# Moving small VectorE work of a fused attention and expert kernel to GpSimd, and scaling early probabilities at their way out of PSUM

## The chip, the cores and the metric

The kernel runs on one core of a Trainium2 chip. Its engines are TensorE (PE in the profile; PEld is its weight load), VectorE (DVE), ScalarE (ACT), GpSimd (POOL) and SyncE (SP), which here only issues transfers. The metric is device microseconds of one launch, the median over several runs; lower is better.

## What is computed

`reference` chains three parts over 4 sequences of 576 tokens with 512 channels.

- **Attention**: 8 heads of 64 channels. Scores are q·k/8 under a block-causal mask (a query sees its own block of 64 and all earlier ones), then a softmax with 1e-9 added to the sum, then the product with v.
- **A dense block** on its result x: `x + relu(layernorm(x) * g @ w_ch1) @ w_ch2`, 512 to 2048 to 512 channels.
- **Experts**: 8 experts of 512 to 1024 to 512 channels; each token takes the expert of the largest logit, or that of the token before it when its local gate says so; the result is scaled by that expert's probability.

## The kernel before

**Numbers.** Operands of TensorE are fp16 pairs: a high half (a cast) and a low half (the fp32 value less the high half). Values v are scaled by V_S = 256, and probabilities by P_S = 256, so that the low halves stay in fp16's range. Before, P_S enters the exponential as LOG_P = ln 256 added to its bias, for every head.

**Tiles.** The 2304 tokens are 18 tiles of 128, in the order 0 to 17. A step s is one tile and one head: 144 steps. The steps of one tile go through `qk` (scores into PSUM), `maxes` (L324 on DVE: scale, mask, row extreme into `sums`; L328 adds LOG_P to the extreme), `exps` (L335 on ACT: exponential, row sums into `sums`), a transposition of the probabilities, and `pv` (times the values). In steps below 30 (`early`: all of tiles 0 to 2, and the first six heads of tile 3) the transposition is done by TensorE in fp32: `emit_turns` transposes into PSUM (L366), ACT writes the high half from there (L369), DVE the low half (L370). In later steps ACT and POOL make the halves (L350, L353, zeros at L352) and a transfer on SP's queue transposes them (L356).

**`finish`** closes a tile after its last `pv`. L408 (DVE) turns the row sums into `(sum + P_S * 1e-9) * V_S`, L411 (DVE) takes the reciprocal, L414 (POOL) multiplies the tile with it. L421 to L426 (DVE) are mean, variance and a first guess of 1/sqrt; L431 (DVE) normalizes by that guess; L435 (ACT) and L436 (POOL) make the halves, and a transfer (L440, SP) transposes them for the dense block. L449 to L468 (DVE) are seven operations on one column that refine the guess to a factor `fac`, read by `post` after the second product.

**Loads and splits.** `load_tile` issues q, k and v of a tile on SP's queue; v has one buffer (`RB = 1`), q and k two. `split_q` and `split_k` make halves on ACT (L237, L244) and POOL (L238, L245; of the first tile on DVE). `split_v` makes the high half on ACT (L252), scaled by V_S, and the low half on DVE (L253, `v * V_S - high` in one operation). They are called in steps 3 and 6 of the tile before.

**Dense weights.** The inputs w_ch1 and w_ch2 are float64. In the first 18 steps `w_next` takes 32 pieces of them: three integer operations on DVE build an fp32 (L198, L202, L205), ACT scales and casts (L218, L219), POOL makes the low half (L223). When a tile group has finished, its dense block is queued in quanta: `l1` (L486 to L488, output halves by ACT L490 and DVE L491) and `l2` (L508 to L510, then `post`, L514 to L526). Quanta are dealt out among the steps by their cost.

**The order.** Every engine works through its own queue in order, and so does each transfer queue. The operations up to the first step are issued in the order of the code; from there to the end of attention a planner that simulates the engines puts each engine's instructions into an order, with priority to tiles 0 and 1 (`HT = 2`). The part after attention (routing and experts) has an order written out by hand for the compute engines.

Of the kernel before, what the change touches and what calls it, by code (L numbers as in the profile page):

```python
# [14 lines left out]
AF = mybir.ActivationFunctionType  # L15
ALU = mybir.AluOpType
# [6 lines left out]
B, H, S, D = 4, 8, 576, 64  # L23
# [11 lines left out]
V_S = 256.0  # L35
P_S = 256.0
LOG_P = math.log(P_S)
# [5 lines left out]
ORDER = [i for ts in GROUPS for i in ts]  # L43
# [47 lines left out]
def kernel(  # L91
# [14 lines left out]
    nc = tc.nc  # L106
# [140 lines left out]
    def split_v(i):  # L247
        r = raw.pop(("v", i))
        o = (KRING + turn_v[0] % VRING) * 1024
        turn_v[0] += 1  # L250
        n = spare[:, o:o + 1024].rearrange("p (h e d) -> p h e d", h=H, e=2)
        nc.scalar.activation(out=n[:, :, 0], in_=r, func=AF.Copy, scale=V_S)  # L252
        nc.vector.scalar_tensor_tensor(  # L253
            out=n[:, :, 1], in0=r, scalar=V_S, in1=n[:, :, 0],
            op0=ALU.mult, op1=ALU.subtract,
        )
        vt[i] = n

    def keys(i):
# [19 lines left out]
    def pack(i):  # L279
        return {1: 2, 2: 2}.get(len(keys(i)), 1)  # L280
# [26 lines left out]
    def early(s):  # L307
        return s < FEW * H - 2

    def maxes(i, h):  # L310
        lo, n = span(i)
        m = pack(i)
        sp = sps.pop((i, h))
        mask = mask_m if i % 9 == 4 else mask_a
        if h % m == 0:
            if early(step[0] + pack(i) - 1):
                sms[i] = ring("ph", [P, 10 * P], F16, 3, MPH).bitcast(F32)
            else:
                sms[i] = ring("sm", [P, 5 * P], F32, 2, MSM)
        sm = sms[i][:, h % m * n:(h % m + 1) * n]  # L320
        if h == 0:
            sums[i] = at.tile([P, 2, H], F32, tag="sums", name="sums", bufs=2)
        nm = sums[i][:, 0, h:h + 1]
        nc.vector.tensor_tensor_reduce(  # L324
            out=sm[:, lo:n], in0=sp[:, lo:n], in1=mask[:, 5 * P - n + lo:5 * P],
            scale=-0.125, scalar=3.0e38, op0=ALU.add, op1=ALU.min, accum_out=nm,
        )
        nc.vector.tensor_scalar(out=nm, in0=nm, scalar1=LOG_P, scalar2=None, op0=ALU.add)  # L328

    def exps(i, h):  # L330
        lo, n = span(i)
# [29 lines left out]
    def emit_turns(upto):  # L361
        while turns and turns[0][0] <= upto:
            _, sm, t, m, k = turns.pop(0)
            tp = sctx["p"].tile([P, 4, P], F32, tag="t", name="ps_t", bufs=2)
            for c in range(m * k):
                nc.tensor.transpose(tp[:, c], sm[:, c * P:(c + 1) * P], eye)  # L366
            tp = tp[:, :m * k].rearrange("p (m k) c -> p m k c", m=m)
            t = t[:, :2 * m * k].rearrange("p (m e k) c -> p m e k c", m=m, e=2)
            nc.scalar.copy(out=t[:, :, 0], in_=tp)  # L369
            nc.vector.tensor_tensor(out=t[:, :, 1], in0=tp, in1=t[:, :, 0], op=ALU.subtract)  # L370

    obs = {}

# [31 lines left out]
    def finish(i):  # L405
        sv = sums.pop(i)
        r = at.tile([P, H], F32, tag="rinv", name="rinv", bufs=2)
        nc.vector.tensor_scalar(  # L408
            out=r, in0=sv[:, 1], scalar1=P_S * 1e-9, scalar2=V_S, op0=ALU.add, op1=ALU.mult
        )  # L410
        nc.vector.reciprocal(out=r, in_=r)  # L411
        ob = obs.pop(i)
        x = wp.tile([P, H, D], F32, tag="x", name="x", bufs=6)
        nc.gpsimd.tensor_tensor(  # L414
            out=x, in0=ob, in1=r[:, :, None].to_broadcast([P, H, D]), op=ALU.mult
        )
        x = x.rearrange("p h d -> p (h d)")
        xt[i] = x
        sm = at.tile([P, 12], F32, tag="lns", name="lns", bufs=2)
        mean, var, y, w = (sm[:, c:c + 1] for c in (6, 7, 8, 9))  # L420
        nc.vector.bn_stats(out=sm[:, 0:6], in_=x)  # L421
        nc.vector.bn_aggr(out=sm[:, 6:8], in_=sm[:, 0:6])
        nc.vector.tensor_scalar(out=var, in0=var, scalar1=LN_EPS, scalar2=None, op0=ALU.add)


        nc.vector.tensor_scalar(  # L426
            out=y.bitcast(I32), in0=var.bitcast(I32), scalar1=-0.5, scalar2=1597463007.0,
            op0=ALU.mult, op1=ALU.add,
        )
        xn = at.tile([P, DM], F32, tag="ob", name="xn", bufs=2)  # L430
        nc.vector.tensor_scalar(  # L431
            out=xn, in0=x, scalar1=mean, scalar2=y, op0=ALU.subtract, op1=ALU.mult
        )
        xh = at.tile([P, 2, DM], F16, tag="nat", name="xh", bufs=2)
        nc.scalar.copy(out=xh[:, 0], in_=xn)  # L435
        nc.gpsimd.tensor_tensor(out=xh[:, 1], in0=xn, in1=xh[:, 0], op=ALU.subtract)  # L436
        g, j, n = group_of(i)
        if j == 0:
            xg[g] = wp.tile([P, 2 * KD, n * P], F16, tag="xg", name="xg", bufs=2)
        nc.sync.dma_start_transpose(  # L440
            out=xg[g][:, :, j * P:(j + 1) * P], in_=xh.rearrange("p e d -> p (e d)")
        )
        if i in GROUPS[-1]:
            c = GROUPS[-1].index(i)
            nc.vector.tensor_copy(stats[:, c, 0:1], mean)
            nc.vector.reciprocal(out=stats[:, c, 1:2], in_=y)

        f = fac[:, i:i + 1]
        nc.vector.scalar_tensor_tensor(  # L449
            out=w, in0=y, scalar=var, in1=y, op0=ALU.mult, op1=ALU.mult  # L450
        )
        nc.vector.tensor_scalar(
            out=f, in0=w, scalar1=-1.0, scalar2=3.0, op0=ALU.mult, op1=ALU.add
        )
        nc.vector.scalar_tensor_tensor(
            out=y, in0=f, scalar=w, in1=f, op0=ALU.mult, op1=ALU.mult
        )
        nc.vector.scalar_tensor_tensor(
            out=f, in0=y, scalar=12.0, in1=f, op0=ALU.subtract, op1=ALU.mult
        )  # L460
        nc.vector.scalar_tensor_tensor(
            out=y, in0=f, scalar=w, in1=f, op0=ALU.mult, op1=ALU.mult
        )
        nc.vector.tensor_scalar(
            out=y, in0=y, scalar1=HOUT / 8192.0, scalar2=HOUT * -3.0 / 32.0,
            op0=ALU.mult, op1=ALU.add,
        )
        nc.vector.tensor_tensor(out=f, in0=f, in1=y, op=ALU.mult)  # L468


    todo = []

# [22 lines left out]
    op = {}  # L495
# [263 lines left out]
    for s in range(nsteps + LAG + MPT):  # L759
# [9 lines left out]
        if s < nsteps:  # L769
            i, h = steps[s]  # L770
# [9 lines left out]
            t = s // H  # L780
# [21 lines left out]
        if queue:  # L802
# [5 lines left out]
            while acc > 0 or s < FREE:  # L808
                n = [x for x in queue if need(x) <= wpos[0] - WREADY]
                n = [x for x in n if x[0] == "l1" or x[1:] == l2_at[0] or x[3] == 0 and l2_free()][:1]  # L810
# [19 lines left out]
    def whole(name, shape, pattern, mult=0, base=0, dt=F32):  # L830
# [17 lines left out]
        out=c_tri16, in_=c_one16, pattern=[[1, P]], compare_op=ALU.is_gt, fill=0.0,  # L848
# [10 lines left out]
    for b in range(B):  # L859
        t, r = divmod(b * S, P)  # L860
# [233 lines left out]
    def third(n):  # L1094
# [14 lines left out]
        out=cand, in0=sub, scalar=0.0, in1=bc(c_rev[:, None, :], NTILE, NE),  # L1109
        op0=ALU.is_equal, op1=ALU.mult,  # L1110
# [6 lines left out]
        out=fresh, in0=z, scalar=0.0, in1=c_first, op0=ALU.is_lt, op1=ALU.max  # L1117
# [15 lines left out]
        out=scan, data0=c_one[:NTILE], data1=pt1[:NTILE, :P], initial=0.0,  # L1133
        op0=ALU.mult, op1=ALU.max,
# [14 lines left out]
        out=car[:, 1:], data0=c_one[:1, :NTILE], data1=pt2[:1, :NTILE], initial=0.0,  # L1149
        op0=ALU.mult, op1=ALU.max,  # L1150
# [14 lines left out]
        out=oh, in0=bc(c_exp[:, :, None], NE, NTILE), in1=bc(ef[:, None, :], NE, NTILE),  # L1165
        op=ALU.is_equal,
# [6 lines left out]
        out=inc.rearrange("p e t -> p (e t)"), data0=c_seg.rearrange("p e t -> p (e t)"),  # L1173
# [6 lines left out]
        out=exc16, in0=inc.rearrange("p e t -> p (e t)"), in1=ohf, op=ALU.subtract  # L1180
    )
    early = GROUPS[last][0]
# [11 lines left out]
        out=lack, in0=pt5[:, NE:NE + 1], scalar1=-1.0, scalar2=128.0, op0=ALU.mult, op1=ALU.add  # L1194
# [5 lines left out]
        out=nti[:, 0:1], in0=pt5[:, 0:1], scalar1=lack, scalar2=127.0, op0=ALU.add, op1=ALU.add  # L1200
# [6 lines left out]
        out=endc, data0=c_one[:, :NE], data1=ntf, initial=0.0, op0=ALU.mult, op1=ALU.add  # L1207
# [6 lines left out]
        out=dst3, in0=pt6[:, :NE * NTILE].rearrange("p (e t) -> p e t", e=NE),  # L1214
        in1=bc(base[:, :, None], NE, NTILE), op=ALU.add,
    )
    V.tensor_scalar(
        out=dst3[:, 0, early:], in0=dst3[:, 0, early:], scalar1=lack, scalar2=None, op0=ALU.add
# [3 lines left out]
    with nc.allow_low_precision("whole numbers"):  # L1222
        V.tensor_reduce(
            out=dst, in_=dst3.rearrange("p e t -> p t e"), axis=AX.X, op=ALU.add
# [21 lines left out]
        out=val[:, :, 0], in0=bc(c_slot[:, None, :], NTILE, NSLOT),  # L1246
        in1=bc(slotf[:, :, None], NTILE, NSLOT), op=ALU.is_equal,
    )
    for n, w in ((1, c_tile), (2, c_row), (3, gh), (4, gl)):
        V.tensor_tensor(  # L1250
            out=val[:, :, n], in0=val[:, :, 0], in1=bc(w[:, :, None], NTILE, NSLOT), op=ALU.mult
# [3 lines left out]
    for t in range(NTILE):  # L1255
        pick = ep.tile([P, P], F16, tag="pick", name="pick", bufs=4)
        V.tensor_scalar(
            out=pick, in0=c_iota, scalar1=rowf[:, t:t + 1], scalar2=None, op0=ALU.is_equal
# [165 lines left out]
```

## Time and profile before

| | us |
|---|---|
| median of 3 runs (lowest, highest) | 811.77 (810.96, 815.51) |
| the profiled execution's own time | 818.86 |
| its span, first to last instruction | 817.2 |
| busy: TensorE, VectorE | 727.9, 431.4 |
| busy: ScalarE, GpSimd | 378.4, 327.9 |

The mean granted TensorE clock is 0.96 of full speed. A window view gives, for stretches of the span, how long each engine was busy; a group view gives one line's instructions of one shape with their number, total and mean time, and behind the bar the idle time of the engine just before them; a timeline gives start and duration of single instructions. Durations in a timeline overlap: a short VectorE instruction is reported somewhat longer than the distance to the start of the next. Attention and the dense block fill the span up to about 520 us, the routing and the experts the rest.

### The profile page before, as it was taken

The numbers are of one execution on the slowest core, as the hardware profiler recorded it, in microseconds if no ns is written. First come the engines' busy times: TensorE is split into PE (matmuls) and PEld (weight loads), VectorE is DVE, ScalarE is ACT, GpSimd is POOL, SyncE is SP. The second block draws the span as 40 slices with busy tenths as digits, with TensorE's granted clock in tenths as the row PEclk, the third lists the DMA queues.
The fourth block names the chain that finished last, engine by engine and source line by source line (L and its number), as shares of the span: only waits on it lengthen the run. The fifth ranks groups of instructions, "written<-read, shape, count | busy, mean of one in ns | idle before, by whom it ended". The sixth has DMA issues, their size and how long they took to land.

```text
span 817.2 us, 16334 instructions
## 1 busy us (share of the span) xinstructions
PE 727.9 (89%) x5598; PEld 435.6 (53%) x5598; DVE 431.4 (53%) x1234; ACT 378.4 (46%) x843; POOL 327.9 (40%) x344
## 2 busy tenths in 40 slices
PE   2559648979998999999999999998997999999995
PEld 1337415676856857656655665455453444444442
DVE  7999986456546467566556653486781111111110
ACT  6878667655546447567554651363051111111110
POOL 3753586756256346566555542300021111111110
PEclk9998778999999999999999999998998999999998
DMA  8874555977478479688966754594025567555663
GB/s 309 294 221 130 155 188 125 222 159 164 63 143 168 124 169 199 117 163 160 194 112 141 120 99 87 180 368 136 14 70 126 124 127 127 121 126 123 131 126 75
DMA packets 240782, 122.60 MB, mean 150 GB/s; under 512 B 220272, under 2 KB 220272, under 8 KB 240688
## 3 DMA queue, kind: packets, MB, share of 16 engines
q1 hardware_dynamic: 233600, 97.05, 55.7%
q10 hardware_dynamic: 3888, 14.16, 5.3%
q0 software_dynamic: 3200, 10.23, 3.9%
q8 instruction: 49, 0.80, 0.4%
q14 instruction: 45, 0.37, 0.1%
HBM read 138.17 MB, written 9.70 MB: 181 GB/s over the span
## 4 chain that ended last, share of the span: by engine, by line
PE 44%; issue 22%; DVE 14%; DMA 12%; POOL 4%; ACT 3%; SPq 1%; POOLq 0%; DVEq 0%; ACTq 0%
DMA out<-eo,dst_i 6%; PE dps L486 6%; PE dps L508 6%; PE dps L509 6%; PE dps L510 6%; PE dps L487 6%; PE dps L488 6%; PE ps_s L298 4%; DMA rawx<-in_k 2%; DVE dps L202 2%; PE ps_o L383 2%; DVE dps L198 2%; DVE sm L324 1%; DVE pt L370 1%; PE ps_o L387 1%
## 5 line engine op out<-in xcount | busy, mean ns | idle before, releaser
L486 PE MATMUL dps<-xg,wide 128*128 128x128 f16 (+2 forms) x576 | 152.6, 278 | 15.8 <-DVE htl L491 10.0
L487 PE MATMUL dps<-xg,wide 128*128 128x128 f16 (+2 forms) x576 | 152.9, 278 | 0.0
L488 PE MATMUL dps<-xg,wide 128*128 128x128 f16 (+2 forms) x576 | 152.8, 278 | 0.0
L353 POOL TENSOR_TENSOR ph<-sm,ph 128x640 f16<-128x640 f32 (+6 forms) x98 | 106.3, 1089 | 94.8 <-ACT ph L350 81.7
L508 PE MATMUL dps<-wide,hth 128*128 128x512 f16 x288 | 111.9, 389 | 8.1 <-ACT wide L219 6.1
L335 ACT ACTIVATE sm<-sm,sums 128x640 f32<-128x640 f32 (+8 forms) x114 | 71.6, 628 | 88.5 <-DVE sums L328 79.4
L509 PE MATMUL dps<-wide,hth 128*128 128x512 f16 x288 | 112.0, 389 | 0.4 <-POOL wide L223 0.4
L1036 DVE SCALAR_TENSOR_TENSOR hth<-hps,hth 128x512 f16<-128x512 f32 x38 | 26.3, 691 | 161.7 <-ACT hth L1035 157.9
L510 PE MATMUL dps<-wide,htl 128*128 128x512 f16 x288 | 111.6, 387 | 0.0
L298 PE MATMUL ps_s<-wide 128*128 128x128 f16 (+4 forms) x560 | 79.0, 269 | 28.4 <-DVE sums L324 16.4
L491 DVE SCALAR_TENSOR_TENSOR htl<-dps,hth 128x128 f16<-128x128 f32 (+2 forms) x144 | 59.5, 417 | 62.2 <-ACT hth L490 62.0
L1062 POOL DMA_INDIRECT out<-eo,dst_i x19 | 19.2, 1013 | 154.9 <-ACT eo L1061 154.9
L487 PEld LDWEIGHTS <-wide 128*128 128x128 f16 x576 | 57.5, 100 | 32.2 <-issue 18.6
L324 DVE CUSTOM_DVE_ANT_0 sm<-ps_s,mask_a 128x192 f32<-128x192 f32 (+7 forms) x98 | 50.9, 531 | 40.3 <-PE ps_s L298 35.6
L490 ACT ACTIVATE hth<-dps 128x128 f16<-128x128 f32 (+2 forms) x144 | 53.6, 379 | 36.6 <-PE dps L488 33.8
L383 PE MATMUL ps_o<-wide,pt 128*128 128x128 f16 x464 | 61.8, 229 | 7.2 <-DVE ob L396 4.7
L298 PEld LDWEIGHTS <-wide 128*128 128x128 f16 x560 | 41.2, 104 | 48.7 <-issue 27.1
L488 PEld LDWEIGHTS <-wide 128*128 128x128 f16 x576 | 57.7, 100 | 15.2 <-issue 0.5
L486 PEld LDWEIGHTS <-wide 128*128 128x128 f16 x576 | 57.6, 100 | 14.9 <-issue 1.0
L387 PE MATMUL ps_o<-wide,pt 128*128 128x64 f16 x464 | 57.3, 201 | 4.2 <-DVE pt L370 4.1
L1035 ACT ACTIVATE hth<-hps 128x512 f16<-128x512 f32 x38 | 22.7, 597 | 79.8 <-PE hps L1018 77.4
L350 ACT CAST ph<-sm 128x640 f16<-128x640 f32 (+6 forms) x98 | 56.2, 579 | 1.4
(264 smaller groups left out, 1516.7 us busy)
## 6 DMA issues: line engine op xcount, KB each, us to landing
raws<-in_moe_w SPq DMA_DIRECT2D x38, 2048.0 KB
raws<-in_moe_w SPq DMA_DIRECT2D x24, 512.0 KB
wraw<-in_moe_w_ch ACTq DMA_DIRECT2D x19, 512.0 KB
rawx<-in_k SPq DMA_DIRECT2D x18, 512.0 KB
rawx<-in_q SPq DMA_DIRECT2D x18, 512.0 KB
raw<-in_v SPq DMA_DIRECT2D x18, 256.0 KB
rows<-x2h SPq DMA_DIRECT2D x18, 256.0 KB
wide<-in_moe_w_ch ACTq DMA_DIRECT2D x8, 512.0 KB
```

Source lines behind the costliest of these rows:

```text
L298: nc.tensor.matmul(sp[:, a * P + o:b * P], lhsT=qt[i, part][:, h], rhs=rhs, start=part == 0 and a % 4 == 0, stop=part == 1 and (b == 4 or ...
L335: nc.scalar.activation(out=e, in_=e, func=AF.Exp, scale=-1.0, bias=sv[:, 0, h:h + 1], accum_out=sv[:, 1, h:h + 1],)
L353: nc.gpsimd.tensor_tensor(out=ph4[:, :, 1, lo:], in0=sm[:, :, lo:], in1=ph4[:, :, 0, lo:], op=ALU.subtract)
L383: nc.tensor.matmul(o, lhsT=t[:, c], rhs=vt[kk][:, h].rearrange("p e d -> p (e d)"), start=c == 0, stop=False,)
L387: nc.tensor.matmul(o[:, 0:D], lhsT=t[:, nk + c], rhs=vt[kk][:, h, 0], start=False, stop=c == nk - 1,)
L486: nc.tensor.matmul(hp, lhsT=wh, rhs=xg[g][:, kk], start=kk == 0, stop=False)
L487: nc.tensor.matmul(hp, lhsT=wh, rhs=xg[g][:, KD + kk], start=False, stop=False)
L488: nc.tensor.matmul(hp, lhsT=wl, rhs=xg[g][:, kk], start=False, stop=kk == KD - 1)
L491: nc.vector.scalar_tensor_tensor(out=hl, in0=hp, scalar=0.0, in1=hh, op0=ALU.max, op1=ALU.subtract)
L508: nc.tensor.matmul(op[j], lhsT=hh, rhs=w2h[:, f], start=f == 0, stop=False)
L509: nc.tensor.matmul(op[j], lhsT=hh, rhs=w2l[:, f], start=False, stop=False)
L510: nc.tensor.matmul(op[j], lhsT=hl, rhs=w2h[:, f], start=False, stop=f == KF - 1)
```

## The change

Four edits. `split_v`: ACT scales v in place in fp32, casts it to the high half in a second operation, and POOL subtracts. `maxes`: the LOG_P addition is left out for the 30 early steps (`plain`), and `emit_turns` multiplies by P_S instead, in the two operations that leave PSUM. `finish`: the sums' operation goes to POOL, in one or two pieces (tile 3 has both kinds of heads), with P_S moved into the factor of the early heads. `finish`: the seven operations of the factor go to POOL, with the column operand given as a scalar of the operation.

```diff
--- before.py
+++ after.py
@@ -249,11 +249,9 @@
         o = (KRING + turn_v[0] % VRING) * 1024
         turn_v[0] += 1
         n = spare[:, o:o + 1024].rearrange("p (h e d) -> p h e d", h=H, e=2)
-        nc.scalar.activation(out=n[:, :, 0], in_=r, func=AF.Copy, scale=V_S)
-        nc.vector.scalar_tensor_tensor(
-            out=n[:, :, 1], in0=r, scalar=V_S, in1=n[:, :, 0],
-            op0=ALU.mult, op1=ALU.subtract,
-        )
+        nc.scalar.activation(out=r, in_=r, func=AF.Copy, scale=V_S)
+        nc.scalar.copy(out=n[:, :, 0], in_=r)
+        nc.gpsimd.tensor_tensor(out=n[:, :, 1], in0=r, in1=n[:, :, 0], op=ALU.subtract)
         vt[i] = n
 
     def keys(i):
@@ -307,6 +305,10 @@
     def early(s):
         return s < FEW * H - 2
 
+    def plain(i, h):
+        m = pack(i)
+        return early(ORDER.index(i) * H + h // m * m + m - 1)
+
     def maxes(i, h):
         lo, n = span(i)
         m = pack(i)
@@ -325,7 +327,8 @@
             out=sm[:, lo:n], in0=sp[:, lo:n], in1=mask[:, 5 * P - n + lo:5 * P],
             scale=-0.125, scalar=3.0e38, op0=ALU.add, op1=ALU.min, accum_out=nm,
         )
-        nc.vector.tensor_scalar(out=nm, in0=nm, scalar1=LOG_P, scalar2=None, op0=ALU.add)
+        if not plain(i, h):
+            nc.vector.tensor_scalar(out=nm, in0=nm, scalar1=LOG_P, scalar2=None, op0=ALU.add)
 
     def exps(i, h):
         lo, n = span(i)
@@ -366,8 +369,11 @@
                 nc.tensor.transpose(tp[:, c], sm[:, c * P:(c + 1) * P], eye)
             tp = tp[:, :m * k].rearrange("p (m k) c -> p m k c", m=m)
             t = t[:, :2 * m * k].rearrange("p (m e k) c -> p m e k c", m=m, e=2)
-            nc.scalar.copy(out=t[:, :, 0], in_=tp)
-            nc.vector.tensor_tensor(out=t[:, :, 1], in0=tp, in1=t[:, :, 0], op=ALU.subtract)
+            nc.scalar.activation(out=t[:, :, 0], in_=tp, func=AF.Copy, scale=P_S)
+            nc.vector.scalar_tensor_tensor(
+                out=t[:, :, 1], in0=tp, scalar=P_S, in1=t[:, :, 0],
+                op0=ALU.mult, op1=ALU.subtract,
+            )
 
     obs = {}
 
@@ -405,9 +411,13 @@
     def finish(i):
         sv = sums.pop(i)
         r = at.tile([P, H], F32, tag="rinv", name="rinv", bufs=2)
-        nc.vector.tensor_scalar(
-            out=r, in0=sv[:, 1], scalar1=P_S * 1e-9, scalar2=V_S, op0=ALU.add, op1=ALU.mult
-        )
+        n = sum(plain(i, h) for h in range(H))
+        for a, b, p in ((0, n, P_S), (n, H, 1.0)):
+            if b > a:
+                nc.gpsimd.tensor_scalar(
+                    out=r[:, a:b], in0=sv[:, 1, a:b], scalar1=P_S / p * 1e-9, scalar2=p * V_S,
+                    op0=ALU.add, op1=ALU.mult,
+                )
         nc.vector.reciprocal(out=r, in_=r)
         ob = obs.pop(i)
         x = wp.tile([P, H, D], F32, tag="x", name="x", bufs=6)
@@ -446,27 +456,17 @@
             nc.vector.reciprocal(out=stats[:, c, 1:2], in_=y)
 
         f = fac[:, i:i + 1]
-        nc.vector.scalar_tensor_tensor(
-            out=w, in0=y, scalar=var, in1=y, op0=ALU.mult, op1=ALU.mult
-        )
-        nc.vector.tensor_scalar(
-            out=f, in0=w, scalar1=-1.0, scalar2=3.0, op0=ALU.mult, op1=ALU.add
-        )
-        nc.vector.scalar_tensor_tensor(
-            out=y, in0=f, scalar=w, in1=f, op0=ALU.mult, op1=ALU.mult
-        )
-        nc.vector.scalar_tensor_tensor(
-            out=f, in0=y, scalar=12.0, in1=f, op0=ALU.subtract, op1=ALU.mult
-        )
-        nc.vector.scalar_tensor_tensor(
-            out=y, in0=f, scalar=w, in1=f, op0=ALU.mult, op1=ALU.mult
-        )
-        nc.vector.tensor_scalar(
+        ts = nc.gpsimd.tensor_scalar
+        ts(out=w, in0=y, scalar1=var, scalar2=y, op0=ALU.mult, op1=ALU.mult)
+        ts(out=f, in0=w, scalar1=-1.0, scalar2=3.0, op0=ALU.mult, op1=ALU.add)
+        ts(out=y, in0=f, scalar1=w, scalar2=f, op0=ALU.mult, op1=ALU.mult)
+        ts(out=f, in0=y, scalar1=12.0, scalar2=f, op0=ALU.subtract, op1=ALU.mult)
+        ts(out=y, in0=f, scalar1=w, scalar2=f, op0=ALU.mult, op1=ALU.mult)
+        ts(
             out=y, in0=y, scalar1=HOUT / 8192.0, scalar2=HOUT * -3.0 / 32.0,
             op0=ALU.mult, op1=ALU.add,
         )
-        nc.vector.tensor_tensor(out=f, in0=f, in1=y, op=ALU.mult)
-
+        ts(out=f, in0=f, scalar1=y, scalar2=None, op0=ALU.mult)
 
     todo = []
```

## Rows read from the trace of the kernel before

**Rows 1.** Windows: busy us of PE, PEld, DVE, ACT, POOL; clock, DMA share, GB/s.

```profile
8.00:28.00 20.00, 8.27 (x46) 5.06 (x47) 19.96 (x59) 14.88 (x37) 10.26 (x7) 1.00 0.91 323
28.00:48.00 20.00, 11.11 (x49) 6.10 (x49) 20.00 (x59) 17.80 (x41) 15.47 (x12) 1.00 0.86 290
48.00:68.00 20.00, 13.38 (x90) 9.01 (x90) 20.00 (x49) 13.66 (x29) 9.48 (x8) 0.87 0.60 190
68.00:88.00 20.00, 18.25 (x249) 15.81 (x248) 19.64 (x68) 16.38 (x48) 5.52 (x5) 0.96 0.34 87
88.00:108.00 20.00, 12.80 (x80) 6.74 (x80) 20.00 (x51) 13.09 (x26) 12.49 (x11) 0.74 0.71 192
108.00:118.00 10.00, 4.87 (x20) 2.12 (x20) 8.72 (x17) 7.25 (x14) 9.92 (x8) 0.80 0.60 188
118.00:175.00 57.00, 44.71 (x512) 32.45 (x511) 30.68 (x95) 33.93 (x86) 38.19 (x33) 0.89 0.81 179
175.00:520.00 345.00, 335.37 (x3046) 223.56 (x3044) 198.33 (x634) 187.87 (x462) 178.93 (x192) 0.99 0.70 137
```

**Rows 2.** Groups by line and shape, DVE, 0 to 118 us.

```profile
L253 DVE SCALAR_TENSOR_TENSOR wide<-raw,wide 128x512 f16<-128x512 f32 x5 | 5.5, 1104 | 0.0
L328 DVE TENSOR_SCALAR sums<-sums 128x1 f32<-128x1 f32 x34 | 4.1, 140 | 0.0
L461 DVE SCALAR_TENSOR_TENSOR lns<-fac,lns 128x1 f32<-128x1 f32 x4 | 3.6, 906 | 0.0
L458 DVE SCALAR_TENSOR_TENSOR fac<-lns,fac 128x1 f32<-128x1 f32 x4 | 3.0, 738 | 0.0
L408 DVE TENSOR_SCALAR rinv<-sums 128x8 f32<-128x8 f32 x4 | 2.0, 504 | 0.0
L468 DVE TENSOR_TENSOR fac<-fac,lns 128x1 f32<-128x1 f32 x4 | 1.9, 463 | 0.0
L449 DVE SCALAR_TENSOR_TENSOR lns<-lns 128x1 f32<-128x1 f32 x4 | 1.7, 430 | 0.0
L455 DVE SCALAR_TENSOR_TENSOR lns<-fac,lns 128x1 f32<-128x1 f32 x4 | 1.0, 247 | 0.0
L452 DVE TENSOR_SCALAR fac<-lns 128x1 f32<-128x1 f32 x4 | 0.6, 139 | 0.0
```

**Rows 3.** Timeline: start us, duration us, engine, line, operation.

```profile
12.59 0.33 DVE L328 TENSOR_SCALAR sums<-sums 128x1 f32<-128x1 f32 x4
...
62.28 2.13 POOL L238 TENSOR_TENSOR wide<-rawx,wide 128x1024 f16<-128x1024 f32 x1 [2.90 <-ACT wide L237]
62.69 1.73 DVE L461 SCALAR_TENSOR_TENSOR lns<-fac,lns 128x1 f32<-128x1 f32 x1
...
75.66 0.20 DVE L461 SCALAR_TENSOR_TENSOR lns<-fac,lns 128x1 f32<-128x1 f32 x1
```

**Rows 4.** Groups by line and shape, whole span: nearest prices for what is added.

```profile
L223 POOL TENSOR_TENSOR wide<-wt,wide 128x512 f16<-128x512 f32 x16 | 19.4, 1215 | 14.4 <-ACT wide L219 12.4 <-DVE dps L198 1.8
L353 POOL TENSOR_TENSOR ph<-sm,ph 128x256 f16<-128x256 f32 x4 | 2.8, 690 | 8.8 <-issue 5.7 <-ACT ph L350 3.0
L858 POOL TENSOR_TENSOR c_tok<-c_tok,c_odd 128x18 f32<-128x18 f32 x1 | 0.2, 218 | 0.0
L853 POOL MEMSET c_seg<- 128x8 f32 x1 | 0.1, 112 | 0.0
L219 ACT CAST wide<-wt 128x512 f16<-128x512 f32 x16 | 9.9, 617 | 0.3
L370 DVE TENSOR_TENSOR pt<-ps_t,pt 128x512 f16<-128x512 f32 x10 | 6.8, 678 | 0.0
L1036 DVE SCALAR_TENSOR_TENSOR hth<-hps,hth 128x512 f16<-128x512 f32 x38 | 26.3, 691 | 161.7 <-ACT hth L1035 157.9 <-ACTq L969 3.8
```

**Rows 5.** Waits (us, times, longest): SP's queue 100 to 175 us, PE 175 to 520 us.

```profile
SPq L167 <- POOL wide L245: 19.2, 5, 12.0
...
PE dps L486 <- DVE htl L491: 4.8, 3, 2.8
```

## The prediction, made before the change was run

> **What bounds the kernel now.** First the busy times by stretch [rows 1]. From 8 to 108 us VectorE is busy 19.6 to 20.0 of every 20 us, while TensorE reaches 8 to 18: VectorE sets the pace. From 108 to 118 us GpSimd takes over (9.92 of 10), and VectorE has 1.3 us to spare. From 118 to 175 us no engine is full (TensorE 44.7 of 57, GpSimd 38.2); there the order of SP's queue counts, whose loads of k wait 19.2 us for GpSimd's low halves of k [rows 5]. From 175 to 520 us TensorE is busy 335.4 of 345: it is the bound, and only 9.6 us of idle time are left to win. Behind 520 us nothing of the change runs. So a microsecond taken from VectorE is worth a microsecond only before 108 us, and only until another engine is full; what is won there is kept, since TensorE's remaining work follows as a block.
>
> Then the groups of VectorE in the first 118 us [rows 2], to see what the moved work costs there. The operations on one column are not cheap: L461 takes 0.906 us on average, L449 0.430. The timeline shows why [rows 3]: the L461 that starts at 62.69 us lasts 1.73 us and ends at 64.42, just after GpSimd's 2.13 us subtraction from 62.28 ends (64.41); the L461 at 75.66, with no GpSimd work beside it, takes 0.20. Part of the VectorE time is thus waiting for GpSimd.
>
> **What leaves VectorE.** Four tiles finish and five v splits run before 118 us. Group totals [rows 2]: L253 5.5, L408 2.0, and the factor's seven operations 1.7 (L449), 0.6 (L452), 1.0 (L455), 3.0 (L458), 3.6 (L461), 0.6 (L464, a repeat of L452's kind) and 1.9 (L468). That makes 19.9 us in 37 instructions. A reported duration overlaps the next start: four L328 in a row fill 0.33 us, so one starts (0.33 - 0.14) / 3 = 0.063 after another although each is reported at 0.14 [rows 2, 3]. I take 0.077 off each: 37 x 0.077 = 2.85, leaving 17.0. The 30 early L328 add 30 x 0.063 = 1.9. Together 18.9 us over the 110 us from 8 to 118, or 3.4 us in each 20.
>
> **What stays at nothing.** In `emit_turns` both operations keep their shape and source and only gain a factor: on VectorE a three-operand form out of PSUM takes 0.691 for 512 columns (L1036) against 0.678 for the two-operand one (L370) [rows 4]; 22 times the difference is 0.3 us at most, and none if the engine has room. On ScalarE I take no difference.
>
> **Where the saving meets a ceiling.** ScalarE gets one more cast of v per tile, 0.617 us (L219, same shape) [rows 4]; two fall in each of the first two stretches. Going through them [rows 1]:
> - 8 to 28: the transfer engines are busy 0.91 of the time, 18.2 us; the weight pieces come no faster. Gain 1.8 of 3.4.
> - 28 to 48: ScalarE 17.8 + 1.2 = 19.0. Gain 1.0.
> - 48 to 68: nothing else is above 14. Gain 3.4.
> - 68 to 88: TensorE is at 18.25. Gain 1.75.
> - 88 to 108: nothing above 13.1. Gain 3.4.
> Sum 11.35 us. Without any ceiling it would be the 18.9.
>
> **What is added to GpSimd.** The v subtraction takes 1.2 us (L223, the same shape) [rows 4]. For the small operations no row shows the form: the ends are 0.11 us (L853, a memset of 8 columns) and 0.69 (L353 at 256 columns, the smallest product of two large operands in the loop); I take 0.22 (L858, 18 columns, two operands), the nearest in kind. A tile gets eight or nine of them. Before 108 us GpSimd has room. From 108 to 118 us it has none: one v subtraction and the factor of one tile, 1.2 + 7 x 0.22 = 2.7 us, lie on the path. With the ends it is 2.0 to 6.0. From 118 to 175 us v is loaded into one buffer, which is now free only after GpSimd's subtraction; behind that load stand the transposing transfers and the k loads on SP's queue. I put one subtraction, 1.2 us, on the path (0 to 4 x 1.2 = 4.8).
>
> **The new wait.** L411 now waits on VectorE for an operation at the end of GpSimd's queue, and everything of VectorE stands behind it. It costs nothing if GpSimd is done in time, as the sums are complete four steps before the tile's last `pv`, and 2.13 us if a k or q subtraction lies in front [rows 3]. For four tiles in the early stage that is 0 to 8.5; I take 1.0, because GpSimd is idle half of that time [rows 1]. The last tile's factor is read only after a whole dense block, so its seven operations cost nothing there.
>
> **Behind 175 us** TensorE's largest wait for VectorE is 4.8 us for L491 [rows 5]. VectorE is at 198 of 345 us and loses some 3 us per tile (14.4 us in four tiles early, without v) [rows 1, 2]; I take 1.5 us back, with ends at 0 and 4.8.
>
> **Sum.** 11.35 - 2.7 - 1.2 - 1.0 + 1.5 = 8.0 us less (7.95). The profiled execution took 818.86 us, so 810.9 in its terms; it lies 7.1 above the median of 811.77, and the saving carried over gives **803.8 us**.
>
> **Rivals.**
> - *No ceiling binds.* ScalarE and the transfers were paced by VectorE themselves and move up with it, and GpSimd's additions fall into gaps. Then the 18.9 come in whole: 792.9. For it: ScalarE's idle time in the first two stretches is short and scattered, which a faster feeder closes. Against: 17.8 of 20.
> - *The wait moves with the work.* Three quarters of L461's cost is waiting for GpSimd, and what waited on one side may be held up on the other: GpSimd's new operations behind VectorE's, L431 behind more GpSimd work. By the undisturbed durations (0.20 for L449, L455, L461, 0.14 for the other four and L408, 0.68 for L253) the 37 instructions cost 4 x (0.6 + 0.7) + 3.4 = 8.6 of their 19.9; 11.3 would stay. The saving is 18.9 - 11.3 = 7.6 over 110 us, 1.4 per stretch and 1.0 where ScalarE binds: 6.6 in all, less 2.7, 1.2 and 1.0, without the gain behind 175 us: 1.7 us less, 810.1. For it: the exact ends in the timeline. Against: the one-column tensor_scalar (L452, 0.139) shows no such wait, so small operations need not meet it.
>  The Trainium skill has this as a rule (Perfetto Trace Analysis, section Optimizing Scalar/DVE Operations): GpSimd and VectorE share an SBUF read port, "so offloading operations between those two might not help". The trace agrees as far as the waits go (1.73 against 0.20 us); no run here shows yet whether GpSimd's small operations pay in turn.
> - *VectorE waits for GpSimd's queue.* Place: L411, in sixteen tiles. GpSimd's operations wait for ScalarE's casts, and in the planner's fixed order one late cast holds the sums' operation, then L411, then L491 and the score operations that TensorE waits for. Price: half a 2.13 us subtraction, 1.07, per tile: 17 us on the end, less 8.0 with its 1.0 of waits put back, or 17 - 9.0 = 8 us slower, 820. It decides from (9.0 + 4.06) / 16 = 0.8 us per tile on. The 0.69 us price for small operations works the same way: nine of them are 6 us in GpSimd's queue per tile. For it: the 19.2 us that SP's loads already wait for GpSimd. Against: GpSimd is at 179 of 345 us behind 175 us.
> - *The saving doesn't reach the path*, because the planner orders the queues anew and the gains meet the stage from 118 to 175 us in another order; its size is that of the second rival, and it is counted there.
>
> **How the numbers follow.** Forecast 0.42, no ceiling 0.20, moved or lost 0.21, the new wait 0.17. A measurement of this kernel tells about 0.5% from no change, so the edges are 807.7 and 815.8 us. Forecast and no ceiling lie below: faster 0.62. The second rival lies between: same 0.21. The third lies above: slower 0.17. The range reaches down to 791.5, just past the case without a ceiling, since more would need both the 18.9 and the gain behind 175 us; up to 816, which leaves out most of the third rival. Outside are some 0.05 below and 0.14 above.
>
> **What would show it.** In the profile after: no SCALAR_TENSOR_TENSOR of 128x1 on VectorE; VectorE below 19.5 of 20 us somewhere before 88 us, with ScalarE nearer to 19 from 28 to 48 us; the last L198 some 8 us earlier; GpSimd's small operations at 0.1 to 0.3 us; the stretch with TensorE saturated starting near 167 instead of 175 us and as long as before. Wrong: idle time before L411 released by GpSimd, above 0.8 us per tile (third rival); L431 or GpSimd's small operations at a microsecond each (second); VectorE still full before 108 us with an early stage as long as before.

## The result and the profile after

The changed kernel takes **804.37 us** (803.77 to 806.75 in four runs) against 813.31 for the kernel before (810.96 to 815.51; one more run beside the three told above); the ratio is 0.9896, 95% interval 0.9857 to 0.9935. The prediction was 803.8, as a saving of 8.0 us from a median of 811.77; measured is 8.5 us by this ratio, from a median 1.5 us higher. In a second set of runs on another occasion it came out at 804.21 against 813.23, ratio 0.9888 (0.9864 to 0.9913), 9.1 us less. Savings in us are worked out from the ratios and 813 to 814 us; differences of the medians can lie up to 2.5 us beside them. The profiled execution of the changed kernel lasted 804.33 us with a span of 802.6; the one before lay some 5 us above its median, so the two traces differ by more (14.6 us of span) than the kernels do.

The stretches of the kernel after, in the columns of [rows 1]:

```profile
8.00:28.00 20.00, 8.54 (x50) 5.49 (x51) 19.39 (x52) 17.21 (x44) 13.62 (x12) 1.00 0.93 349
28.00:48.00 20.00, 11.30 (x58) 7.11 (x57) 20.00 (x49) 19.62 (x45) 17.14 (x16) 0.75 0.87 296
48.00:68.00 20.00, 16.68 (x165) 12.68 (x164) 18.07 (x48) 17.32 (x43) 15.72 (x21) 0.74 0.72 219
68.00:88.00 20.00, 13.17 (x199) 11.78 (x197) 18.71 (x50) 14.94 (x41) 10.42 (x18) 0.94 0.45 94
88.00:108.00 20.00, 12.19 (x67) 5.45 (x67) 16.18 (x31) 14.65 (x26) 16.43 (x13) 0.84 0.78 236
108.00:118.00 10.00, 5.52 (x36) 2.95 (x36) 6.11 (x16) 6.38 (x13) 9.18 (x11) 0.58 0.99 231
118.00:175.00 57.00, 49.57 (x645) 38.50 (x644) 27.11 (x105) 37.77 (x103) 42.29 (x48) 0.97 0.75 152
175.00:520.00 345.00, 334.29 (x2939) 219.16 (x2938) 155.20 (x495) 189.46 (x453) 218.22 (x323) 0.99 0.71 146
```

VectorE is no longer full in most stretches: of each 20 us it has 0.6 to spare from 8 to 28 us, 1.9 from 48 to 68, 1.3 from 68 to 88 and 3.8 from 88 to 108; before, it had at most 0.4 in any of the five up to 108 us [rows 1]. From 28 to 48 us it still is, and there ScalarE is full beside it, 19.62 of 20 instead of 17.80. The last row must be read with care: attention ends earlier now, so its last 14 us belong to the next part.

How much earlier a fixed place is reached is seen from the first integer operation of the weight pieces (L198) and from the first operation of the routing (L1104). A single line asked for gives: engine, operation, count, shortest/median/longest ns, first to last start. Before:

```profile
L198 DVE TENSOR_SCALAR dps<-wraw x22: 666/681/696, 8.6 to 130.3; 128x512 int32<-128x512 int32 x22
L1104 DVE TENSOR_TENSOR sub<-lg,mx x1: 307/307/307, 569.5 to 569.5; 128x144 f32<-128x144 f32 x1
```

After, and the first of the two once more from a second profile of the same kernel (the run after_again below):

```profile
L198 DVE TENSOR_SCALAR dps<-wraw x22: 676/687/704, 8.7 to 120.2; 128x512 int32<-128x512 int32 x22
L1104 DVE TENSOR_TENSOR sub<-lg,mx x1: 308/308/308, 555.8 to 555.8; 128x144 f32<-128x144 f32 x1
...
L198 DVE TENSOR_SCALAR dps<-wraw x22: 680/690/696, 8.6 to 123.9; 128x512 int32<-128x512 int32 x22
```

The weights are done 10.1 us earlier and the routing starts 13.7 us earlier; in the second profile it is 6.4 and 12.8 us (the routing at 556.7). From there to the end both need the same: 817.2 - 569.5 = 247.7 us and 802.6 - 555.8 = 246.8. All but 0.9 us of the difference is won in attention and the dense block beside it. How much of that is won in the first 120 us the profiles do not settle: 10.1 of 13.7 us by one, 6.4 of 12.8 by the other. TensorE did about as much from 8 to 118 us as before (67.4 us of busy time, and 67.0 in the second profile, against 68.7); it did more from 118 to 175 us (49.6 and 50.1 against 44.7).

What the moved work costs on GpSimd, by the groups of the kernel after (columns as in [rows 4]; L417 is the sums' operation, L460 to L469 the factor's seven, L254 the values):

```profile
L254 POOL TENSOR_TENSOR wide<-raw,wide 128x512 f16<-128x512 f32 x18 | 20.8, 1158 | 12.1 <-ACT wide L253 12.1
L460 POOL TENSOR_SCALAR lns<-lns 128x1 f32<-128x1 f32 x18 | 8.2, 454 | 5.5 <-DVE lns L436 5.3
L464 POOL TENSOR_SCALAR lns<-fac,lns 128x1 f32<-128x1 f32 x18 | 6.1, 340 | 1.1
L462 POOL TENSOR_SCALAR lns<-fac,lns 128x1 f32<-128x1 f32 x18 | 6.1, 340 | 3.6 <-DVE sums L331 2.9
L463 POOL TENSOR_SCALAR fac<-lns,fac 128x1 f32<-128x1 f32 x18 | 5.6, 311 | 1.9
L469 POOL TENSOR_SCALAR fac<-fac,lns 128x1 f32<-128x1 f32 x18 | 5.2, 291 | 1.3
L417 POOL TENSOR_SCALAR rinv<-sums 128x8 f32<-128x8 f32 (+2 forms) x19 | 3.9, 206 | 5.9 <-ACT sm L338 3.1 <-ACT ph L338 1.5
L461 POOL TENSOR_SCALAR fac<-lns 128x1 f32<-128x1 f32 x18 | 3.9, 215 | 0.4
L465 POOL TENSOR_SCALAR lns<-lns 128x1 f32<-128x1 f32 x18 | 3.6, 200 | 0.8
```

The seven sum to 2.15 us per tile. On VectorE, two lines changed that were not moved: the normalization (L431 before, L441 after) and the reciprocal (L411 before, L421 after), which now waits. By the groups of the kernel before, then of the kernel after:

```profile
L431 DVE TENSOR_SCALAR xn<-x,lns 128x512 f32<-128x512 f32 x18 | 18.2, 1013 | 0.4
L411 DVE RECIPROCAL rinv<-rinv 128x8 f32<-128x8 f32 x18 | 3.5, 197 | 0.2
...
L441 DVE TENSOR_SCALAR xn<-x,lns 128x512 f32<-128x512 f32 x18 | 24.8, 1378 | 0.5
L421 DVE RECIPROCAL rinv<-rinv 128x8 f32<-128x8 f32 x18 | 3.6, 200 | 7.8 <-POOL rinv L417 7.7
```

The normalization took 18.2 us in 18 operations before and takes 24.8; the reciprocal's idle time was 0.2 us and is 7.8.

### The profile page after: what moved, and what is told of

Same layout as the page of the kernel before. It is cut to its first block, busy times and chain, and to the rows that moved or that the text cites. A ratio compares the mean times of both kernels' runs of the same rounds, so it can differ in the third digit from the quotient of the medians.

```text
span 802.6 us, 16294 instructions
## 1 busy us (share of the span) xinstructions
PE 716.6 (89%) x5598; PEld 431.4 (54%) x5598; DVE 368.2 (46%) x1042; ACT 385.2 (48%) x861; POOL 387.0 (48%) x507
## 4 chain that ended last, share of the span: by engine, by line
PE 39%; issue 21%; DMA 17%; POOL 8%; ACT 7%; DVE 6%; SPq 1%; POOLq 0%; ACTq 0%; DVEq 0%
DMA out<-eo,dst_i 6%; PE dps L508 6%; PE dps L509 6%; PE dps L510 6%; PE dps L486 5%; PE dps L488 5%; PE dps L487 5%; DMA rawx<-in_k 4%; PE ps_s L296 3%; DMA raw<-in_v 2%; POOL wide L245 2%; PE ps_o L389 2%; POOL ph L356 1%; DMA wraw<-in_moe_w_ch 1%; ACT wide L244 1%
## 5 line engine op out<-in xcount | busy, mean ns | idle before, releaser
L296 PE MATMUL ps_s<-wide 128*128 128x128 f16 (+4 forms) x560 | 76.4, 262 | 26.2 <-DVE sums L326 12.7
L491 DVE SCALAR_TENSOR_TENSOR htl<-dps,hth 128x128 f16<-128x128 f32 (+2 forms) x144 | 60.0, 420 | 85.4 <-ACT hth L490 85.0
L487 PEld LDWEIGHTS <-wide 128*128 128x128 f16 x576 | 57.4, 100 | 29.3 <-issue 15.6
L978 POOL DMA_INDIRECT xg<-rows,src_i x21 | 21.9, 1043 | 80.5 <-DVE src_i L1272 59.9
```

The lines of the kernel that those rows point to most:

```text
L296: nc.tensor.matmul(sp[:, a * P + o:b * P], lhsT=qt[i, part][:, h], rhs=rhs, start=part == 0 and a % 4 == 0, stop=part == 1 and (b == 4 or ...
L487: nc.tensor.matmul(hp, lhsT=wh, rhs=xg[g][:, KD + kk], start=False, stop=False)
L491: nc.vector.scalar_tensor_tensor(out=hl, in0=hp, scalar=0.0, in1=hh, op0=ALU.max, op1=ALU.subtract)
```

## The experiments

Twelve kernels ran, in three sets; each set has its own runs of the kernel before on the same chip, and ratios are to those.

**One part alone: the factor on GpSimd.** The kernel before with only this edit:

```diff
-        nc.vector.scalar_tensor_tensor(
-            out=w, in0=y, scalar=var, in1=y, op0=ALU.mult, op1=ALU.mult
-        )
...
+        ts = nc.gpsimd.tensor_scalar
+        ts(out=w, in0=y, scalar1=var, scalar2=y, op0=ALU.mult, op1=ALU.mult)
...
```

> Only the seven operations of the factor go to GpSimd; all else as before. Theory A (VectorE time before 118 us is what pays, and most of it was waiting for GpSimd): 12.4 us of group time less 28 x 0.077 = 10.2 us leave VectorE there; with the ceilings of the prediction (about 0.6 of it comes through) 5 to 7 us less, ratio 0.991 to 0.994. Rival B (the wait moves with the work; GpSimd's small operations or L431 pay instead): within 2 us of before, and GpSimd's small operations at 0.5 us or more each. Rival C (the planner's new order, not the moved time, made the gain): no relation to the 10.2 us, and the parts run alone do not add up to the whole.

Measured: 808.18 us, ratio 0.9922 (0.9892 to 0.9952), 6.3 us less than before, as theory A said. Rival B's "within 2 us" is out, and so are its 0.5 us or more for each small operation: they take 0.19 to 0.48 us on GpSimd. Little of the wait moved: the seven had taken 54.4 us of VectorE in 18 tiles, and there the values' subtraction (L253) grew by 2.9 us and the sums' operation (L408) by 1.5.

**One part alone: the values on GpSimd.** Only `split_v` as in the change.

```diff
-        nc.scalar.activation(out=n[:, :, 0], in_=r, func=AF.Copy, scale=V_S)
-        nc.vector.scalar_tensor_tensor(
...
+        nc.scalar.activation(out=r, in_=r, func=AF.Copy, scale=V_S)
+        nc.scalar.copy(out=n[:, :, 0], in_=r)
+        nc.gpsimd.tensor_tensor(out=n[:, :, 1], in0=r, in1=n[:, :, 0], op=ALU.subtract)
```

> Only the values' lower halves go to GpSimd, with ScalarE's second operation; all else as before. Theory A: 5.5 us less 5 x 0.077 = 5.1 us leave VectorE before 118 us, but ScalarE gets 5 x 0.62 us and GpSimd 5 x 1.2 us, and the single buffer of v is free later: 0 to 3 us less, ratio 0.996 to 1.000. Rival B: as the subtraction holds GpSimd longer, VectorE's other waits grow by as much: 0 or up to 2 us more. Rival C: any size.

Measured: 809.95 us, ratio 0.9966 (0.9939 to 0.9992), 2.8 us less. Part of the wait did move here, as rival B has it: the subtraction had taken 19.1 us of VectorE in 18 tiles, and the normalization slowed from 1.013 to 1.286 us on average, 4.9 us in 18, the factor's first operation from 0.590 to 0.733, 2.6 us.

**One part alone: the sums on GpSimd and the early scaling.** `maxes`, `emit_turns` and the sums' operation as in the change, values and factor as before.

```diff
-        nc.vector.tensor_scalar(out=nm, in0=nm, scalar1=LOG_P, scalar2=None, op0=ALU.add)
+        if not plain(i, h):
+            nc.vector.tensor_scalar(out=nm, in0=nm, scalar1=LOG_P, scalar2=None, op0=ALU.add)
```

> Only the sums' operation on GpSimd and the early probabilities scaled at their way out of PSUM; factor and values as before. Theory A: L408 2.0 us less 0.3 and 30 x 0.063 us of L328, 3.6 us of VectorE before 118 us: 1 to 3 us less, ratio 0.996 to 0.999; L421's wait for GpSimd at 0.2 to 0.5 us per tile. Rival D (VectorE waits for GpSimd's queue at the reciprocal): 0 to 5 us more, the reciprocal idle 0.8 us or more per tile.

Measured: 811.76 us, ratio 0.9982 (0.9959 to 1.0005). Its 1.5 us fit theory A, but the interval reaches past 1, so no saving is shown. The reciprocal's idle time is 3.9 us in 18 tiles, 0.2 us each, far from rival D's 0.8.

The three ratios multiply to 0.9871, the whole change has 0.9896 and 0.9888: within the intervals the parts add, with perhaps 1 to 2 us lost between them. Rival C, a lucky order, has little support: the parts rank as their VectorE time in the first 118 us does (10.2, 5.1 and 3.6 us of it gave 6.3, 2.8 and 1.5). It isn't excluded. The planner's order does differ between these kernels: the sixth of the 18 reciprocals runs at 157.2 us in the kernel before and later, at 165.9, in the changed kernel, though the eighth runs earlier there, at 216.0 instead of 229.7. No run here held the order fixed.

**The wait alone: the factor stays on VectorE in another form.** The kernel before, with

```diff
-        nc.vector.scalar_tensor_tensor(
-            out=w, in0=y, scalar=var, in1=y, op0=ALU.mult, op1=ALU.mult
-        )
...
+        ts = nc.vector.tensor_scalar
+        ts(out=w, in0=y, scalar1=var, scalar2=y, op0=ALU.mult, op1=ALU.mult)
...
```

> The seven operations of the factor stay on VectorE, but in the form that the changed kernel uses (the second column given as a scalar of the operation, not as a second tensor); all else as before. Theory A, in its part on the wait (a VectorE operation waits for GpSimd when it reads a second tensor; the one-column tensor_scalar L452 at 0.139 us never does): every one of the seven at 0.13 to 0.22 us on average, some 12.4 - 28 x 0.15 = 8 us less of VectorE before 118 us without a single instruction moved, and 3 to 6 us less in all. If the wait comes with any small operation on SBUF: L449, L458 and L461 stay at 0.4 to 0.9 us on average, time as before. Rival B says the same time as before in both cases.

Measured: 803.94 us, ratio **0.9912** (0.9885 to 0.9939), 7.2 us less (9.6 by the medians), as much as moving it (0.9922), and no instruction has moved to another engine. The seven operations on VectorE, first 118 us, by the groups (columns as in [rows 2]; L450 to L459 answer to L449 to L468 there):

```profile
L450 DVE TENSOR_SCALAR lns<-lns 128x1 f32<-128x1 f32 x4 | 1.1, 269 | 0.0
L452 DVE TENSOR_SCALAR lns<-fac,lns 128x1 f32<-128x1 f32 x4 | 1.1, 266 | 0.0
L454 DVE TENSOR_SCALAR lns<-fac,lns 128x1 f32<-128x1 f32 x4 | 1.0, 261 | 0.0
L453 DVE TENSOR_SCALAR fac<-lns,fac 128x1 f32<-128x1 f32 x4 | 0.8, 208 | 0.0
L459 DVE TENSOR_SCALAR fac<-fac,lns 128x1 f32<-128x1 f32 x4 | 0.8, 202 | 0.0
L451 DVE TENSOR_SCALAR fac<-lns 128x1 f32<-128x1 f32 x4 | 0.6, 146 | 0.0
L455 DVE TENSOR_SCALAR lns<-lns 128x1 f32<-128x1 f32 x4 | 0.6, 144 | 0.0
```

They take 6.0 us where the same arithmetic took 12.4 [rows 2]: L461's 0.906 us is 0.261 here (L454), L458's 0.738 is 0.208 (L453). The longest ones came out at 0.26 to 0.27 and not below 0.22 as written, but the wait is gone: in all 18 tiles none of the seven takes more than 0.29 us, where L461 took up to 1.98 before. For these one-column operations it belongs to the second tensor operand, not to small operations as such. One tensor operand isn't enough in every shape: in the same kernel the sums' operation on eight columns (L408) takes 0.15 to 1.67 us and the normalization of 512 columns (L431) 0.54 to 2.29. This part of the change could have been had without GpSimd.

The Trainium skill names the mechanism (SBUF — State Buffer, section Who interferes with whom): a VectorE instruction with two SBUF inputs contends with a GpSimd instruction that reads SBUF, and one with at most one SBUF input, outside the two-port modes, does not. The trace agrees for these one-column operations: 0.26 against 0.91 us.

**The changed kernel again, and the factor's form in it.** The second set starts from the changed kernel. Alone once more:

> The changed kernel once more, so that the three runs beside it can be set against it on the same chip. Theory A: ratio to before 0.987 to 0.993. If the parts simply added (0.992, 0.997 and 0.998 each alone) it would be 0.987; with ceilings between them 0.990.

Measured: 804.21 us, ratio 0.9888 (0.9864 to 0.9913). With the factor back on VectorE in the new form (`ts = nc.vector.tensor_scalar` for `nc.gpsimd.tensor_scalar`):

> The changed kernel with the factor's seven operations back on VectorE, in the form with the second column as a scalar. Theory A (the factor's part was waiting, and the form alone ends it): VectorE gets 4 x 7 x 0.12 = 3.4 us before 118 us, GpSimd loses 2.15 us per tile; the wait of L421 and of the normalization for GpSimd become shorter. 0 to 4 us less than the changed kernel. Rival E (moving the work off VectorE is what counts): 2 to 4 us more than the changed kernel.

Measured: 802.82 us, ratio 0.9877 (0.9852 to 0.9901): 1.4 us less than the changed kernel, inside the interval. That speaks against rival E, which had it 2 to 4 us slower. With the sums' operation on VectorE too:

> As after_factor_column_scalar, and the sums' operation back on VectorE too, so that of the change only the values on GpSimd and the early scaling remain. Theory A: L421's wait of 7.7 us is gone, L408's own wait (2.0 us in four tiles before) is back; within 2 us of after_factor_column_scalar. Rival D: 3 to 6 us less than it.

Measured: 805.17 us, ratio 0.9891 (0.9861 to 0.9921), not told apart from the other two. No idle time is left before the reciprocal for GpSimd, and no time was won. But the wait isn't all that changed: the sums' operation takes 0.690 us on VectorE on average, 13.1 us in all, and itself waits for ScalarE (6.2 us idle in all). Rival D's 3 to 6 us less did not come; the next run tests the wait from the other side.

**Is GpSimd's queue on the path?** Each of the factor's operations is done twice on GpSimd, as in

```diff
         ts(out=w, in0=y, scalar1=var, scalar2=y, op0=ALU.mult, op1=ALU.mult)
+        ts(out=z, in0=y, scalar1=var, scalar2=y, op0=ALU.mult, op1=ALU.mult)
...
```

> The changed kernel with each of the factor's seven operations on GpSimd done twice, the second time into a spare column that nothing reads: 2.15 us more per tile on GpSimd, 39 us in all, of which 9 before 118 us and 4 from there to 175 us. Theory A: GpSimd has room except from 96 to 175 us; 1 to 4 us more than the changed kernel. Rival D (GpSimd's queue holds up VectorE and SP): 8 us more or above, with longer idle time before L421.

Measured: 803.16 us, ratio 0.9867 (0.9841 to 0.9892). No more than the changed kernel within about a microsecond (0.9888 there), though the reciprocal's idle time rose from 7.7 to 11.9 us. Both theories are off here, A by less: the factor on GpSimd costs nothing that can be measured, not even from 108 to 118 us, where GpSimd is 9.2 of 10 us busy. Rival D falls: the new wait exists, and 4.2 us more of it did not reach the end.

**How much is a microsecond of VectorE worth, before and after?** The first integer operation of every second weight piece is done twice, in the kernel before and in the changed one:

```diff
+        for _ in range(2 - p % 2):
-        nc.vector.tensor_scalar(
+            nc.vector.tensor_scalar(
...
```

> The kernel before, with the first integer operation of every second weight piece done twice on VectorE: 16 x 0.60 = 9.6 us more on VectorE in the first 130 us, none of it waiting for GpSimd. Theory A (VectorE sets the pace there): 7 to 11 us more than before, ratio 1.009 to 1.013. If VectorE were not the bound: under 4 us.

> The same 9.6 us of VectorE added to the changed kernel. Theory A with the ceilings of the prediction (other engines and transfers are close behind VectorE once it is relieved): 3 to 7 us more than the changed kernel, less than the same addition costs before. Rival F (no ceiling binds; VectorE is still the only bound early): 9 to 10 us more, as before.

Measured: before, 818.43 us, ratio 1.0070 (1.0041 to 1.0098), 5.7 us for the 9.6 added, or 0.6 of it (3.3 to 8.0 us by the interval). In the changed kernel 807.13 us, ratio 0.9913 (0.9881 to 0.9946) against the 0.9888 of the unaltered one in the set before: 2.0 us, 0.2 of what was added, with some 3 us of uncertainty. So VectorE did set the pace before, at about 0.6 to one, below the 7 to 11 us expected; after the change the point lies at 0.2, below the 3 to 7 expected. Rival F's 9 to 10 us are out. That a microsecond of VectorE is worth less after the change than before is likely and not quite shown: the two slopes differ by 3.7 us, with some 4 us of uncertainty. The planner's order differs here too (the sixth reciprocal at 179.5 us in the kernel before with the added work, 157.2 without).

**What is full now? ScalarE's second operation on v taken away.**

```diff
-        nc.scalar.activation(out=r, in_=r, func=AF.Copy, scale=V_S)
-        nc.scalar.copy(out=n[:, :, 0], in_=r)
+        nc.scalar.activation(out=n[:, :, 0], in_=r, func=AF.Copy, scale=V_S)
         nc.gpsimd.tensor_tensor(out=n[:, :, 1], in0=r, in1=n[:, :, 0], op=ALU.subtract)
```

> The changed kernel without ScalarE's second operation on v (18 x 0.62 us, five of them before 118 us): the high half is written at once and GpSimd subtracts it from the unscaled v, so the low halves of v are not those of the reference, with the same work otherwise. Theory A with ScalarE as the ceiling from 28 to 48 us: 0.5 to 2 us less than the changed kernel. Without that ceiling: the same within 0.5 us.

Measured: 835.98 us, ratio 1.0264 (1.0223 to 1.0306). This total says nothing on the cast: with other values the tokens choose other experts, and the part from the routing on is 832.6 - 549.2 = 283.4 us long instead of 246.8, with 20 blocks of results written instead of 19. Attention can still be compared. The start of the routing in this kernel, in the columns of the L1104 rows above:

```profile
L1103 DVE TENSOR_TENSOR sub<-lg,mx x1: 309/309/309, 549.2 to 549.2; 128x144 f32<-128x144 f32 x1
```

It is at 549.2 us against 555.8 in the changed kernel and 556.7 in its second profile. That is about 7 us by single profiles, more than the 0.5 to 2 expected, and the planner's order differs too; the direction fits a full ScalarE, the size is not settled by one profile.

**A faster version.** The cast can leave ScalarE without a change of values: GpSimd scales v itself, and the factor stays on VectorE in the new form.

```diff
-        nc.scalar.activation(out=r, in_=r, func=AF.Copy, scale=V_S)
-        nc.scalar.copy(out=n[:, :, 0], in_=r)
+        nc.scalar.activation(out=n[:, :, 0], in_=r, func=AF.Copy, scale=V_S)
+        nc.gpsimd.tensor_scalar(out=r, in0=r, scalar1=V_S, scalar2=None, op0=ALU.mult)
...
-        ts = nc.gpsimd.tensor_scalar
+        ts = nc.vector.tensor_scalar
```

> A candidate for a faster kernel: the changed kernel with the factor on VectorE in the column-scalar form, and the scaling of v for the low half on GpSimd in place of ScalarE's extra cast (one more GpSimd operation of 512 columns, about 0.6 us, in place of 0.62 us on ScalarE). Theory A: GpSimd has the room that the factor left; 9 to 12 us less than before, ratio 0.985 to 0.989, and within 2 us of the changed kernel with the column-scalar factor. If GpSimd's queue is what now counts: 2 us more than that one.

Measured: **798.97 us**, ratio 0.9808 (0.9758 to 0.9858), the shortest of all, 15.6 us less than before, beyond the 9 to 12 expected, and some 7 less than the changed kernel (0.9888 and 0.9896). The routing starts at 549.7 us. GpSimd is up to 19.5 of 20 us busy between 28 and 48 us, by the windows of this kernel in the columns of [rows 1]:

```profile
28.00:48.00 20.00, 13.87 (x73) 8.69 (x72) 20.00 (x50) 19.26 (x45) 19.52 (x16) 1.00 0.86 284
```

TensorE does 13.87 us of work there instead of 11.30 and 12.27 in the two profiles of the changed kernel. ScalarE's share is hardly lower, 19.26: it is still close to full, with 45 operations as before and without the two casts. The interval of this kernel and that of after_factor_column_scalar (0.9852 to 0.9901) overlap by a little, and the two stood in different sets; that the cast cost time is thus likely by both runs, and shown by neither alone. Here the cast's place is taken by work on GpSimd, so the gain is that of the exchange.

## Why the prediction was right

The time came within 0.6 us of the forecast, the saving within 0.5 to 1.2 us (8.5 and 9.1 against 8.0), and the mechanism holds: VectorE set the pace early, and part of its time was waiting. The terms fit less well than their sum, so the closeness is in part luck.

- **VectorE bounds the early stage, and part of its time is waiting.** Shown: 9.6 us more of VectorE cost 5.7 us before, and taking only the wait out of the factor (6.4 us of VectorE in the first 118) gave 7.2 us (5.0 to 9.4).
- **The share that comes through.** The ceilings let through 11.35 of 18.9 us, 0.60. The measured shares scatter about that: the factor on GpSimd gave 6.3 of 10.2 us, the factor in the other form 7.2 of 6.4, so 0.6 is no constant of the kernel. That added work came through at 5.7 / 9.6 = 0.6 too does not bear out the ceilings: they limit what a saving brings, and by them added work should have cost nearly all of its 9.6 us. Why it cost less stays open. The ceiling named for 28 to 48 us is there: ScalarE 19.62 where 19.0 was worked out, though VectorE is full beside it, so this row alone does not tell which of them binds. The one for 68 to 88 us is not: TensorE has 13.17 and not 18.25 there, since the work moved between stretches; a ceiling read from a stretch of the old kernel holds only as long as the same work falls into it.
- **GpSimd's additions.** The small operations were put at 0.22 us; they take 0.20 to 0.45, 2.15 per tile against 1.54. The 2.7 us that were put on the path from 108 to 118 us held one v subtraction and one factor. The factor's share was wrong: doubling it cost nothing that can be measured. The subtraction's share was not tried by itself.
- **The new wait.** The sum had 1.0 us for four tiles before 118 us, by 0.25 each; in the trace the reciprocal waited 0.5 us once there. Over all tiles it waited 7.7 us, 0.43 each, below the 0.8 from which it was to decide, and lengthening it to 11.9 cost nothing that can be measured.
- **Behind 175 us.** 1.5 us were to come back. The wait of TensorE for L491 fell from 4.8 us in three to this, by the waits of TensorE in the kernel after, 175 to 505 us:

```profile
PE dps L486 <- DVE htl L491: 1.3, 2, 1.0
```

From 175 to 500 us TensorE is busy 317.3 us and was 315.4, 1.9 us more by one profile each. With the factor in the other form on VectorE it is 319.4, so part of that form's gain lies here and not in the early stage.
- **From 118 to 175 us.** The sum had only a cost here, 1.2 us. TensorE does 4.9 us more work in this stretch than before (5.4 in the second profile), the largest increase of any row; it seems that what was won earlier arrives here.
- **The rivals.** "No ceiling binds" (18.9 us) is out by the result itself, and by the slope of 0.2 in the changed kernel. "The wait moves" is half true: the normalization pays 6.6 us in 18 tiles, and GpSimd's L460 takes 0.454 us where its like (L462) takes 0.340; with the values alone moved, 7.5 of their 19.1 us came back in two lines of VectorE. For the factor alone, 0.9922, most of the saving stays. The sentence of the Trainium skill quoted in the prediction (Perfetto Trace Analysis, section Optimizing Scalar/DVE Operations) says that offloading between the two "might not help". In this case it did help: the factor alone on GpSimd brought 6.3 us, though its other form on VectorE brought as much without offloading.

Errors of opposite sign met in the sum: too much was charged for GpSimd and the new wait (up to 4.9 us together), and the cast on ScalarE was charged with 1.2 us in one stretch, where the two runs without it point to several, neither of them settling the size.

## What to carry to other kernels

When an engine is full, look first at the instructions that take longer than their size asks: the same operation at 0.20 and at 1.73 us tells of a wait inside the duration, and a form with one tensor operand may end it without moving any work, as it did here for one column. Before work is moved to an engine, add it to that engine's busy time in the same stretch, and do the same for every helper operation that the move needs: here the extra cast on ScalarE stood in the fullest stretch. To learn whether an engine sets the pace, add a known amount of harmless work to it; what of it arrives at the end gives a first guess of what a saving of that size can bring. It is no more than that: here 0.6 of the added work arrived, and the savings that are shown brought 0.5 to 1.1 of the VectorE time that they took away.

## What was not expected of the hardware

A one-operand multiplication of 128x512 fp32 on GpSimd, in place, takes longer than the two-operand subtraction of the same columns (which writes fp16), and more than twice the 0.6 us that its expectation gave. By the groups of the fastest kernel:

```profile
L253 POOL TENSOR_SCALAR raw<-raw 128x512 f32<-128x512 f32 x18 | 26.9, 1497 | 17.6 <-ACT wide L252 17.4
L254 POOL TENSOR_TENSOR wide<-raw,wide 128x512 f16<-128x512 f32 x18 | 21.0, 1169 | 0.2
```

GpSimd's one-column operations grow with the columns given as scalars: 0.20 us with none (L465), 0.29 and 0.31 with one (L469, L463), 0.34 with two (L462, L464); L460, also with two, takes 0.33 to 0.61.

And the granted clock: in the first profile of the changed kernel TensorE had 0.75 and 0.74 of its 2.4 GHz from 28 to 68 us, so about half of the time at 1.2, while it was busy 11 to 17 of 20 us; in the second, with the same program, it stayed at the upper level:

```profile
28.00:48.00 20.00, 12.27 (x59) 7.36 (x58) 20.00 (x48) 19.49 (x46) 17.34 (x16) 1.00 0.89 307
48.00:68.00 20.00, 13.70 (x111) 10.04 (x110) 14.03 (x35) 13.16 (x32) 12.21 (x13) 1.00 0.88 194
```

The spans were 802.6 and 803.2 us: where TensorE waits for other engines anyway, half a stretch at the lower level cost nothing that can be seen between these two. In the kernel before it may be otherwise: of 19 executions the four shortest (810.0 to 810.2 us) had a mean granted clock of 0.970 to 0.978, the two longest (817.9 and 820.1) 0.960 and 0.952. Whether the lower clock made them longer, or longer waits the lower clock, no run here shows.
